# A third seven-product unit in tile 2, its x sums moved to the end of tile 1, and another PSUM bank for two value products of the prologue

## The chip, the cores and the metric

One Trainium2 chip, one core. The metric is device time of one execution in microseconds (us); medians are given with the lowest and highest run. A "profile" is one traced execution; its span is about 2 us shorter than the timed figure of the same run. Engines: PE is TensorE, DVE is VectorE, ACT is ScalarE, POOL is GpSimd.

## The reference

Shortened; x, the input of the second part, is the output of the first, put together over the heads.

```python
def _attn_ref(q, k, v):                       # 8 batches, 8 heads, 576 rows, 64 wide
    k_p = k.reshape(B, H, Sp, 8, D).mean(axis=3)      # keys and values pooled by 8
    v_p = v.reshape(B, H, Sp, 8, D).mean(axis=3)
    scores = scale * np.matmul(q, k_p.transpose(0, 1, 3, 2))
    ...                                               # softmax over the 72 pooled rows
    return np.matmul(attn, v_p)

def _moe_ref(x, w_in, w_out):                 # x: 4608 tokens x 512; d_ff = 2048
    h = x @ w_in
    g = h * (1.0 / (1.0 + np.exp(-h)))        # Silu
    return g @ w_out
```

## The kernel before

The tokens go through in nine tiles of 512. Tile t has an *up* phase (x @ w_in and Silu into `h_T`) and a *down* phase (times w_out), and beside the down phase the attention of batch t + 1. All matmuls are bf16, but for some of the warm-up. (Tile 4, and tile 0 for most groups, cut the 512 columns in two.)

An up phase has sixteen groups of 128 hidden columns. A plain group is four matmuls of 512 columns. A *unit* does four groups at once with Strassen's scheme: seven products of four 256-column matmuls, on sums of weights (`w_sum`, made once) and of tokens (`x_sum`, made per tile). Its outputs are put together by VectorE:

```python
elif n == "5":
    product(y, 5, "Q", True)
    tt(out=rr_sb, in0=ps[y, "Q"], in1=r_sb, op=ALU.add)
elif n == "1":
    product(y, 1, "R", True)
    tt(out=t_sb, in0=ps[y, "R"], in1=rr_sb, op=ALU.subtract)
...
elif n == "7":
    product(y, 7, "P", False)
    tt(out=c_sb[0], in0=ps[y, "P"], in1=t_sb, op=ALU.add)     # then a Silu from c_sb
```

The program fixes for each engine the order in which its instructions are issued, and the traces show VectorE keeping to it: in e4 below it sat idle for 1.73 us before one instruction, while sums that had run at this point of the tile in the kernel before stood behind it. `f_up` and `f_down` are lists of (step, piece of work): the piece is issued when the matmuls of the phase have come to that step:

```python
if t < 3:
    for n in U_X:
        f_up.append((0, lambda n=n: unit_x_sum(t, n)))        # x sums first thing in the tile
for n in (2, 5):
    h_at = 50 if t == B else 54 if t > 2 else 45
    f_up.append((h_at, lambda n=n: hidden_sum(n, 4, 8)))      # token sums of h_T for the down phase
...
else:                                                         # t > 1
    f_up.append((1, behind_x_sums))       # a GpSimd copy that reads x_sum: holds POOL until they are done
    f_up.append((1, lambda: pool_k(a)))   # two GpSimd adds
    ...
    f_up.append((2, lambda: pool_v(a)))   # two more
```

The kernel takes its PSUM tiles, into which the matmuls write, from two pools of banks: three (`mm`) and five (`at`). Each pair of value products of the prologue (the work before the first hidden matmul) takes one of each, each set of scores four of the five.

The softmax here doesn't subtract the row's maximum and nothing guards it: scores larger than these inputs give would overflow.

## Time and profile before

282.61 us (282.60 to 282.72, three runs). The first hidden matmul starts at 16.2 us and the rest of tile 0 lasts 34.9 us. Tile 0 has no unit, tile 1 one, tile 2 two, tiles 3 to 8 three.

### The profile page before, as it was taken

What the parts mean: (1) busy time and instruction counts of PE and PEld (TensorE: products, weight loads), DVE (VectorE), ACT (ScalarE), POOL (GpSimd) and SP (SyncE); (2) the same over time, 40 slices, a digit from 0 to 9 for tenths busy, and PEclk for the clock granted to TensorE, in tenths of its full rate; (3) what the DMA queues carried; (4) which work ended last, traced back from release to release, by engine and by line L of the source; (5) the groups of instructions that cost most, each with busy time, mean ns of one, the idle gap of its engine ahead of it and who ended that gap; (6) DMA issues with size and microseconds to landing.
All of it is one profiled execution on the core that took longest, in us unless ns stands there. A gap on an engine that the chain in (4) does not pass through costs nothing.

```text
span 280.5 us, 7088 instructions
## 1 busy us (share of the span) xinstructions
PE 275.4 (98%) x2853; PEld 201.4 (72%) x2853; DVE 218.2 (78%) x409; ACT 187.7 (67%) x365; POOL 98.7 (35%) x104
## 2 busy tenths in 40 slices
PE   8999999999999999999999999999999999999995
PEld 4448444556777578867888878787877778788684
DVE  4886746889887876897689768885888588966983
ACT  1688765668677776797579857984799578326700
POOL 8745217332138630863077106970640000000001
PEclk9999999999999999999999999999999999999999
DMA  7999999795659769569755944699610041004104
GB/s 210 284 260 238 210 325 171 227 197 94 148 72 203 200 108 170 129 181 132 138 132 154 135 65 121 141 144 139 160 26 2 0 105 49 0 11 109 33 4 148
DMA packets 31312, 37.70 MB, mean 134 GB/s; under 512 B 10352, under 2 KB 22256, under 8 KB 31280
## 3 DMA queue, kind: packets, MB, share of 16 engines
q0 software_dynamic: 23920, 27.03, 51.7%
q1 hardware_dynamic: 6928, 9.58, 12.4%
q10 hardware_dynamic: 432, 0.66, 0.6%
q8 instruction: 22, 0.36, 0.5%
q14 instruction: 10, 0.08, 0.1%
HBM read 36.70 MB, written 9.44 MB: 164 GB/s over the span
## 4 chain that ended last, share of the span: by engine, by line
PE 82%; DMA 12%; DVE 3%; issue 1%; ACT 1%; DVEq 0%
PE o_psP L645 15%; PE o_psQ L645 15%; PE hp_ps L537 13%; PE u_psP L477 10%; PE u_psQ L477 10%; PE o_psR L645 5%; DMA w_out_sb<-in_moe_w_out_dram 5%; DMA raw<-in_k_dram 4%; DMA q_bf<-in_q_dram 3%; PE u_psR L477 3%; PE sc_ps L340 3%; PE nu_ps L384 2%; PE warm_ps L694 2%; PE den_ps L358 2%; PE warm_ps L698 1%
## 5 line engine op out<-in xcount | busy, mean ns | idle before, releaser
L645 PEld LDWEIGHTS <-h_sum 128*128 128x128 bf16 x640 | 60.4, 98 | 13.1 <-DVE h_sum L605 2.7
L537 PE MATMUL hp_ps<-xT,w_in_sb 128*128 128x512 bf16 (+3 forms) x300 | 58.1, 337 | 0.1
L605 DVE TENSOR_TENSOR h_sum<-h_T 128x1024 bf16<-128x1024 bf16 (+1 forms) x72 | 51.9, 771 | 1.0 <-ACT h_T L543 1.0
L477 PEld LDWEIGHTS <-w_sum 128*128 128x128 bf16 x420 | 41.1, 98 | 7.7
L543 ACT ACTIVATE h_T<-hp_ps 128x512 bf16<-128x512 f32 (+2 forms) x71 | 36.3, 528 | 12.9 <-PE hp_ps L537 11.7
L348 ACT ACTIVATE es<-sc_ps 72x384 bf16<-72x384 f32 (+1 forms) x100 | 39.1, 470 | 8.8 <-PE sc_ps L340 8.7
L537 PEld LDWEIGHTS <-w_in_sb 128*128 128x128 bf16 x300 | 28.6, 98 | 18.4 <-issue 1.1
L485 ACT ACTIVATE h_T<-c_sb 128x512 bf16<-128x512 f32 x42 | 26.1, 627 | 4.9 <-DVE c_sb L509 4.3
L393 DVE TENSOR_TENSOR xT<-nu_ps,rec 128x384 bf16<-128x384 f32 (+1 forms) x50 | 24.0, 532 | 4.3 <-PE nu_ps L384 4.3
L645 PEld LDWEIGHTS <-h_T 128*128 128x128 bf16 x256 | 24.1, 98 | 4.5 <-issue 0.9
L549 POOL DMA_DIRECT2D out_dram<-o_sb x2 | 1.2, 618 | 68.3 <-issue 67.6
L367 ACT ACTIVATE lnd<-den_ps 128x384 f32<-128x384 f32 (+1 forms) x23 | 11.1, 484 | 19.7 <-PE den_ps L358 19.7
L190 POOL TENSOR_TENSOR raw<-raw 72x1024 f32<-72x1024 f32 x10 | 23.6, 2360 | 0.1
L500 DVE TENSOR_TENSOR t_sb<-u_psR,rr_sb 128x512 f32<-128x512 f32 x21 | 14.5, 692 | 6.7 <-PE u_psR L477 4.8
L494 ACT COPY r_sb<-u_psP 128x512 f32<-128x512 f32 x21 | 12.3, 584 | 10.1 <-PE u_psP L477 8.7
L263 DVE TENSOR_TENSOR raw<-raw 128x384 f32<-128x384 f32 (+3 forms) x20 | 12.4, 618 | 8.5 <-DMA raw<-in_v_dram 4.9
L645 PE MATMUL o_psP<-w_out_sb,h_sum 128*128 128x256 bf16 x128 | 17.7, 273 | 0.6 <-DVE h_sum L605 0.6
L477 PEld LDWEIGHTS <-w_in_sb 128*128 128x128 bf16 x168 | 16.1, 98 | 2.6
L497 DVE TENSOR_TENSOR rr_sb<-u_psQ,r_sb 128x512 f32<-128x512 f32 x21 | 14.3, 681 | 3.7 <-ACT r_sb L494 2.1
L509 DVE TENSOR_TENSOR c_sb<-u_psP,t_sb 128x512 f32<-128x512 f32 x21 | 14.4, 687 | 3.1 <-ACT h_T L485 1.4
L196 POOL COPY gate<-x_sum 1x1 bf16<-1x1 bf16 x5 | 0.9, 180 | 44.9 <-DVE x_sum L444 44.9
L645 PE MATMUL o_psQ<-w_sum,h_sum 128*128 128x256 bf16 x128 | 16.7, 273 | 0.0
(84 smaller groups left out, 518.6 us busy)
## 6 DMA issues: line engine op xcount, KB each, us to landing
out_dram<-o_sb SPq DMA_DIRECT2D x128, 64.0 KB, 1.8
raw<-in_k_dram POOLq DMA_DIRECT2D x10, 576.0 KB, 8.1
raw<-in_v_dram POOLq DMA_DIRECT2D x10, 576.0 KB, 7.8
q_bf<-in_q_dram POOLq DMA_DIRECT2D x6, 576.0 KB, 10.9
w_in_sb<-in_moe_w_in_dram POOLq DMA_DIRECT2D x8, 256.0 KB, 8.5
w_out_sb<-in_moe_w_out_dram POOLq DMA_DIRECT2D x4, 512.0 KB, 13.2
raw<-in_v_dram POOLq DMA_DIRECT2D x2, 768.0 KB, 11.0
raw<-in_k_dram POOLq DMA_DIRECT2D x1, 768.0 KB, 10.7
```

The costliest lines, as they stand in the source:

```text
L190: nc.gpsimd.tensor_add(out=raw[:, :, : 2 * D], in0=raw[:, :, : 2 * D], in1=raw[:, :, 2 * D :])
L348: nc.scalar.activation(es[:, s, :], sc[s], func=AF.Exp, scale=score_scale)
L393: nc.vector.tensor_mul(out=xT[:, 2 * g0 + c : 2 * (g0 + ng - 1) + c + 1 : 2, cols], in0=nu[c][:, :w].rearrange("r (g n) -> r g n", g=ng), ...
L477: nc.tensor.matmul(ps[y, bank][:, u, :], lhsT=w[:, kk, 128 * u : 128 * (u + 1)], rhs=x[:, kk, :], start=first and u == 0 and kk == 0, stop ...
L485: nc.scalar.activation(h_T[:, g : g + 2, j * NQ : (j + 1) * NQ], src, func=AF.Silu)
L497: tt(out=rr_sb, in0=ps[y, "Q"], in1=r_sb, op=ALU.add)
L500: tt(out=t_sb, in0=ps[y, "R"], in1=rr_sb, op=ALU.subtract)
L509: tt(out=c_sb[0], in0=ps[y, "P"], in1=t_sb, op=ALU.add)
L537: nc.tensor.matmul(hp_ps[:, r0:r1], lhsT=w_in_sb[:, kk, g * 128 : (g + 1) * 128], rhs=xT[:, kk, x0 : x0 + r1 - r0], start=(kk == 0), stop= ...
L543: nc.scalar.activation(h_T[:, g, n0 : n0 + n], hp_ps[:, :n], func=AF.Silu)
L605: nc.vector.tensor_tensor(out=h_sum[n][:, ks, :], in0=quarter(*a, ks), in1=quarter(*b, ks), op=op)
L645: nc.tensor.matmul(ps[b][:, c, :], lhsT=left(n, kt, c), rhs=W_OUT[n][:, kt, :], start=b not in begun, stop=kt == k1 - 1, skip_group_check= ...
```

## The change

Its intent: give tile 2 the third unit that tiles 3 to 8 have, with their whole schedule, and let the prologue's scores not wait for a bank.

```diff
-    numerators(0, part(1, 0), ("mm", "at"))
+    numerators(0, part(1, 0), ("mm", "mm"))
...
-            elif t > 2:
+            else:
                 items = []
                 for it in THREE[t // B].split(): ...          # the three-unit order
-            else:
-                items = ( ... two units ... )
-            if t < 3:
+            if t == 1:
                 for n in U_X:
                     f_up.append((0, lambda n=n: unit_x_sum(t, n)))
             for n in (2, 5):
-                h_at = 50 if t == B else 54 if t > 2 else 45
+                h_at = 50 if t == B else 54 if t > 1 else 45
...
-            q_at = [4, 14, 4, 8] if t > 2 else [15, 16, 17, 8] if t > 1 else ...
+            q_at = [4, 14, 4, 8] if t > 1 else ...
...
-        if 1 < t < B:
+        if 0 < t < B:
             for n in (4, 1, 3, 7, 6):
                 f_down.append((98 if t < B - 1 else 44, lambda n=n: unit_x_sum(t + 1, n)))
```

More of the change, by code (lines that the diff above doesn't have):

```diff
@@ L815 @@
                     items += [(("BCA".index(it[0])), it[1])] if it[0] in "ABC" else G(int(it[1]))
-            else:
-                items = (
-                    G(12, 13) + [(0, "251")] + G(14) + [(0, "43")] + G(15) + [(0, "76")]
-                    + [(1, "2")] + [(0, "hs")] + [(1, "51")] + G(0) + [(1, "43")] + G(1)
-                    + [(1, "7h6")] + G(2) + [(1, "s")] + G(3)
-                )
-            if t < 3:
+            if t == 1:
                 for n in U_X:
@@ L842 @@
         if a < B:
-            q_at = [4, 14, 4, 8] if t > 2 else [15, 16, 17, 8] if t > 1 else [24, 25, 26, 2] if t else [82, 84, 86, 88]
+            q_at = [4, 14, 4, 8] if t > 1 else [24, 25, 26, 2] if t else [82, 84, 86, 88]
             if t == 0:
@@ L867 @@
             for n in range(4):
-                f_to = f_down if t and n >= (2 if t > 2 else 3) else f_up
+                f_to = f_down if t and n >= (2 if t > 1 else 3) else f_up
                 f_to.append((q_at[n], lambda n=n: q_transpose(a, n % 2, n // 2)))
```

## The prediction

> **What bounds the kernel now.** I read four things in this order: the page's busy shares, the waits of TensorE, a table of windows cut at the nine token tiles, and the timelines of the two places that the change touches. The page first:
>
> ```profile
> PE 275.4 (98%) x2853; PEld 201.4 (72%) x2853; DVE 218.2 (78%) x409; ACT 187.7 (67%) x365; POOL 98.7 (35%) x104
> ```
>
> 98% of a 280.5 us span alone proves little, because matmul ends are modelled and overlap. So I ask for TensorE's waits:
>
> ```profile
> engine line waited for: us in total, times, longest us
> PE warm_ps L694 <- DVE warm L713: 1.2, 1, 1.2
> PE o_psP L645 <- DVE h_sum L605: 0.6, 1, 0.6
> ```
>
> Only two waits are left. The first is the start of the program. The second is one single event, and the PE timeline puts it at 97.63 us, in the second half of tile 2. Starts of consecutive matmuls say the rest: a 256-column product starts every 0.109 us and a 512-column one every 0.216 us, and apart from changes of operation nothing departs from this for long. So from about 16 us to the end the kernel is a queue on TensorE, and a change is worth what it takes out of that queue.
>
> I then cut the span where the matmuls of a new token tile begin (columns: stretch and its length, then busy us and count for PE, PEld, DVE, ACT, POOL; clock, DMA share, GB/s). The rows are tiles 1, 2, 3 and 4:
>
> ```profile
> 51.10:81.35 30.25, 30.20 (x318) 20.19 (x317) 26.41 (x60) 21.94 (x41) 9.17 (x9) 1.00 0.68 142
> 81.35:111.62 30.27, 29.62 (x314) 21.39 (x312) 23.41 (x39) 21.41 (x42) 12.98 (x10) 1.00 0.87 166
> 111.62:140.35 28.73, 28.73 (x326) 22.66 (x324) 23.31 (x42) 22.12 (x43) 12.65 (x10) 1.00 0.74 146
> 140.35:169.10 28.75, 28.75 (x342) 24.18 (x340) 23.28 (x42) 22.11 (x43) 11.90 (x9) 1.00 0.60 121
> ```
>
> This table carries the prediction. Tile 2 takes 30.27 us, and tiles 3 and 4, which have three seven-product units already, take 28.73 and 28.75. (Some matmul records are missing, so counts are not compared.) Tile 2 has 0.65 us in which PE was not busy, tile 3 none.
>
> Why does tile 2 wait? Its PE, DVE and POOL timelines, then DVE at the same place of tile 3:
>
> ```profile
> 97.63 1.05 PE L645 MATMUL o_psP<-w_out_sb,h_sum 128*128 128x256 bf16 x8 [0.65 <-DVE h_sum L605]
> 99.48 0.67 PE L358 MATMUL den_ps<-es,ones 72*32 72x384 bf16 x4
> ```
> ```profile
> 90.76 3.33 DVE L605 TENSOR_TENSOR h_sum<-h_T 128x1024 bf16<-128x1024 bf16 x2
> 94.01 0.68 DVE L509 TENSOR_TENSOR c_sb<-u_psP,t_sb 128x512 f32<-128x512 f32 x1
> ```
> ```profile
> 89.48 2.37 POOL L190 TENSOR_TENSOR raw<-raw 72x1024 f32<-72x1024 f32 x1
> 91.94 1.60 POOL L193 TENSOR_TENSOR vp<-raw 72x512 bf16<-72x512 f32 x1
> ```
> ```profile
> 123.53 4.29 DVE L605 TENSOR_TENSOR h_sum<-h_T 128x1024 bf16<-128x1024 bf16 x7
> ```
>
> In tile 2 two hidden sums took 3.33 us, 1.67 each; in tile 3 seven took 4.29, 0.61 each. The slow pair lies beside GpSimd's two pooling adds. Behind it the unit's last c_sb starts at 94.01; ScalarE sat idle 2.03 us for that c_sb, finished its last Silu at 96.84, and the sums that the down product needs began at 96.88. That is the 0.65 us. The two ragged denominators at 99.48 (0.67 us against 0.35 elsewhere) are its tail, since the exponentials come after those Silus on ScalarE.
>
> **What the Trainium skill says.** "SBUF — State Buffer", section "Who interferes with whom": a VectorE instruction with two SBUF inputs contends with a GpSimd instruction that reads SBUF, and the one that comes second is blocked. A hidden sum is such an instruction, and the trace agrees: 1.67 us beside the adds against 0.61 alone. "TensorE: Matmul & The Clock Gate", section "Wait — 56ns, not 53.3ns?": a warm matmul costs N / 2.4 GHz and about 2.5 ns, that is 109.2 ns for 256 columns and 215.8 for 512. The trace agrees (0.109 and 0.216; granted clock 1.00 in every tile). "PSUM — Partial Sum Buffer", section "PSUM bank collisions raise a hardware error": a bank must be guarded by semaphores whole, not by address. So a matmul into a recycled bank waits for its last reader; the prologue shows that below.
>
> **The change part by part.**
>
> *1. Third unit in tile 2.* A unit replaces four hidden groups of four 512-column matmuls: 16 x 0.2158 = 3.45 us. It has seven products of four 256-column matmuls: 28 x 0.1092 = 3.06 us. TensorE is saved 0.39 us. The two up phases say the same: tile 2 goes from 81.35 to its first down product at 94.50, 13.15 us; tile 3 from 111.62 to 124.37, 12.75 us; 0.40 apart. It adds four VectorE operations of about 0.69 us (rr, t and two c) and one ScalarE copy of 0.58; the four plain Silus become four of 0.60 to 0.63. None of this lies on PE's path if the order holds, and the order is tile 3's, where the same load of 23.3 us VectorE and 22.1 us ScalarE runs with no PE wait.
>
> *2. Hidden sums from step 45 to step 54.* They now follow the last c_sb, as in tile 3, some 11.9 us after the tile's start: 93.3 on the clock of before. GpSimd's adds end at 93.54 now, but they hang behind a gate that waits for the x sums (POOL was idle 4.07 us for it). With the x sums a part of tile 1 that gate opens about 1.45 us earlier, so the adds should end near 91.8. Sums and adds no longer meet. So the wait (0.65 as idle, 0.81 by start-to-start: 0.918 instead of 0.107) goes, and with it the ragged denominators, 0.33. Parts 1 and 2 together: 0.40 + 0.81 + 0.33 = 1.54 us, just what the table gives: 30.27 - 28.73 = 1.54.
>
> *3. x sums at the end of tile 1.* Five VectorE operations, 1.75 us for all, unchanged in number. They now stand between the last xT products (done 80.79) and the last output sum, which moves from 81.55 to about 82.4. It holds an output bank, which the next tile's later groups need; tile 3 starts with the same order (xT done 0.56 us before its first matmul, as also here) and shows no wait. PE time: 0.
>
> *4. Prologue.* The second value product pair goes into two banks of the three, so that it takes no bank of the five. The rows of now (ScalarE, PE, ScalarE):
>
> ```profile
> 14.54 1.30 ACT L348 ACTIVATE es<-sc_ps 72x288 bf16<-72x288 f32 x4
> ```
> ```profile
> 15.12 1.17 PE L340 MATMUL sc_ps<-qT,kz 32*72 32x288 bf16 x8
> ```
> ```profile
> 16.24 1.30 ACT L348 ACTIVATE es<-sc_ps 72x288 bf16<-72x288 f32 x4 [0.40 <-PE sc_ps L340]
> 17.56 1.28 ACT L403 ACT_TABLE_LOAD   x1
> ```
>
> Eight score matmuls took 1.17 us where the same eight take 0.45 elsewhere. The starts of the first four are 0.17, 0.30 and 0.30 us apart, in step with the four exponentials that free their banks (each new one 0.30 after the last): bank for bank they wait for all four. With one more bank free they wait for the first three alone, so the fourth starts one exponential, 0.30 us, earlier. The hidden products behind it (16.23) follow, and so do the exponentials, the table load and the Silus that a later value product waits for: everything moves by about 0.29 us. Its own operands allow it: the xT products it needs end at 16.02 and are first used after the denominators; the first input-weight halves have landed by 15.1, as the queue's waits show.
>
> Sum: 282.61 - 1.54 - 0.29 = **280.78 us**.
>
> **The rivals.**
> *The prologue's gain is absorbed.* In tile 0 data from memory come at fixed times: the value rows are summed after a 4.9 us DMA wait, and the output weights land just in time. If one of these were the limit, PE would wait there and the 0.29 would go. For: the chain of waits runs through DMA up to 46 us. Against: PE shows no wait there; value sums are done 1.9 to 2.5 us before PE uses them, and the last quarter of the output weights, issued at 26.54 and given the longest landing of 15.7 us, is there at 42.24, about 0.6 us before its use. The result would be 281.1.
> *Only the arithmetic goes, a wait stays.* If the sums still meet GpSimd's adds (the load between the adds, or a late value row, holds these), or tile 1's fuller VectorE (26.4 us against 23.3) hands on a delay, tile 2 keeps part of its 1.14 us and the result is 281.3 to 281.9. Against: in tile 1 VectorE sat idle 0.92 and 0.76 us near its end, so it is not behind.
> *The new order makes PE wait*, for x sums or an output bank: 283 at worst. Against: the x sums end near 82.4, and their first product comes some 2.2 us after the tile's start, at 83.5, as in tile 3.
>
> **Range and chances.** The centre is 280.8 because two separate readings of tile 2 (parts, and tile 3 as a twin) agree. The range runs from 280.4 (all of it and some rounding) to 281.5 (prologue absorbed and part of the wait kept); 2% would be 5.65 us, over three times the whole gain, so "faster by over 2%" has 1%, slower 1%, within 98%.
>
> **What would show each step.** Tile 2, between first matmuls, should last 28.7 to 28.8 us, and its up phase 12.75. TensorE's wait for h_sum should be gone from the waits, VectorE's hidden sums of tile 2 should last 0.61 us each, and the gate should run about 1.4 us earlier within its tile. The eight scores should take about 0.87 us, the first hidden product should start near 15.94, and tile 1 should begin near 50.8 instead of 51.1. I am wrong on the prologue if tile 1 still begins at 51.1, and wrong on tile 2 if a PE wait for h_sum, x_sum or u_ps is left or new.

## More of the kernel before

The experiments ran in three sets on three chips (e1, e2, e3, e7; e4, e5, e6, e8; e9 to e12), each set with the kernel before run beside it.

## The result

280.56 us (280.25 to 281.55, six runs) against 282.61 of before (282.29 to 282.82, six runs). The ratio is 0.9933, 95% interval 0.9917 to 0.9950: the mean time of the runs of one kernel over that of the other's in the same rounds, so not quite the ratio of the medians. The interval is clear of 1, and the change is, as forecast, well within 2%. A later control, in another set of runs, gave 280.68 and 0.9942.

The waits of TensorE in the changed kernel (same columns as before):

```profile
PE warm_ps L694 <- DVE warm L713: 1.2, 1, 1.2
PE kz_ps L285 <- DVE k L267: 0.8, 1, 0.8
```

The wait for `h_sum` is gone. The second line lies before 8 us, where the first key rows come in; it differs from run to run. Tiles 1, 2 and 3 by windows:

```profile
50.94:81.17 30.23, 30.17 (x318) 20.22 (x317) 26.95 (x62) 21.95 (x41) 9.18 (x9) 1.00 0.71 146
81.17:109.90 28.73, 28.73 (x326) 22.65 (x324) 23.30 (x42) 22.12 (x43) 12.67 (x10) 1.00 0.90 176
109.90:138.63 28.73, 28.73 (x326) 22.64 (x324) 23.30 (x42) 22.12 (x43) 12.68 (x10) 1.00 0.72 141
```

Tile 2 is now its sister's twin in length and in VectorE, ScalarE and GpSimd time. GpSimd in tile 2, then VectorE:

```profile
82.35 0.18 POOL L196 COPY gate<-x_sum 1x1 bf16<-1x1 bf16 x1 [3.64 <-DVE x_sum L444]
...
87.88 2.39 POOL L190 TENSOR_TENSOR raw<-raw 72x1024 f32<-72x1024 f32 x1
90.34 1.27 POOL L193 TENSOR_TENSOR vp<-raw 72x512 bf16<-72x512 f32 x1
```
```profile
93.07 4.29 DVE L605 TENSOR_TENSOR h_sum<-h_T 128x1024 bf16<-128x1024 bf16 x7
```

The gate runs 1.18 us after the tile's start instead of 2.63. The adds end at 91.61, the sums begin at 93.07 and take 0.61 each. The prologue, on TensorE:

```profile
14.99 0.88 PE L340 MATMUL sc_ps<-qT,kz 32*72 32x288 bf16 x8
15.80 0.42 PE L537 MATMUL hp_ps<-xT,w_in_sb 128*128 128x288 bf16 x2
```

The eight scores take 0.88 us for 1.17, and hidden work starts 0.81 us after the first score, not 1.11. But tile 1 starts at 50.94, only 0.18 us earlier than in the profile of before. Where did the rest of that 0.3 go? TensorE's timeline in tile 0's down phase, before and then after:

```profile
41.79 1.68 PE L572 MATMUL o_ps<-w_out_sb,h_T 128*128 128x512 bf16 x7
43.31 0.34 PE L303 MATMUL v_ps<-v,shifts 128*128 128x64 bf16 x6
```
```profile
41.36 1.94 PE L572 MATMUL o_ps<-w_out_sb,h_T 128*128 128x512 bf16 x7
43.14 0.34 PE L303 MATMUL v_ps<-v,shifts 128*128 128x64 bf16 x6
```

The same seven matmuls take 0.26 us more. By single starts it is one gap: 0.476 us from 42.23 to 42.71 where 0.216 is the pace, and the matmul behind it is the first that waits for the semaphore of the last quarter of w_out. It does not show among the waits, because the modelled end of the matmul before covers 0.16 of it and the view leaves out the 0.10 that remain. The last quarter's landing is the longest of the four in the view of `w_out_sb`, before and then after:

```profile
DMA to landing us min/median/max: 11.9/13.2/15.7
```
```profile
DMA to landing us min/median/max: 11.9/13.3/16.1
```

It was issued at 26.54 and 26.57, so it was there at 42.22 before (used at 42.88) and at 42.67 after (used at 42.71). So TensorE, now earlier, ran into a transfer.

Summed over the two profiled runs: 0.18 us before tile 1, none in tile 1, 1.54 in tile 2, none in tiles 3 to 7, and 0.15 at the very end (see the last section but one): 1.87 us, the difference of the spans (280.53 and 278.66). Of the 0.18, 0.13 was there before the eight scores began (14.99 against 15.12), so it is not the bank's doing.

### The profile page after: what moved, and what is told of

The parts are those of the page before. It is cut to its first block, busy times and chain, and to the rows that moved or that the text cites. A ratio compares the mean times of both kernels' runs of the same rounds, so it can differ in the third digit from the quotient of the medians.

```text
span 278.7 us, 7121 instructions
## 1 busy us (share of the span) xinstructions
PE 273.3 (98%) x2865; PEld 201.9 (72%) x2865; DVE 218.7 (78%) x413; ACT 188.4 (68%) x366; POOL 98.7 (35%) x104
## 4 chain that ended last, share of the span: by engine, by line
PE 81%; DMA 12%; POOL 2%; DVE 2%; issue 1%; DVEq 0%; POOLq 0%
PE o_psP L645 16%; PE o_psQ L645 16%; PE hp_ps L537 12%; PE u_psP L477 10%; PE u_psQ L477 10%; DMA w_in_sb<-in_moe_w_in_dram 6%; DMA w_out_sb<-in_moe_w_out_dram 6%; PE o_psR L645 5%; PE u_psR L477 3%; PE sc_ps L340 3%; PE nu_ps L384 2%; PE den_ps L358 2%; DVE w_sum L623 1%; POOL q_bf L133 1%; DVE xT L393 1%
## 5 line engine op out<-in xcount | busy, mean ns | idle before, releaser
L537 PE MATMUL hp_ps<-xT,w_in_sb 128*128 128x512 bf16 (+3 forms) x284 | 54.1, 334 | 0.1
L605 DVE TENSOR_TENSOR h_sum<-h_T 128x1024 bf16<-128x1024 bf16 (+1 forms) x72 | 49.7, 742 | 0.0
L477 PEld LDWEIGHTS <-w_sum 128*128 128x128 bf16 x440 | 43.1, 98 | 7.8
L543 ACT ACTIVATE h_T<-hp_ps 128x512 bf16<-128x512 f32 (+2 forms) x67 | 33.8, 524 | 11.5 <-PE hp_ps L537 10.5
L537 PEld LDWEIGHTS <-w_in_sb 128*128 128x128 bf16 x284 | 27.1, 98 | 17.1 <-issue 1.1
L485 ACT ACTIVATE h_T<-c_sb 128x512 bf16<-128x512 f32 x44 | 27.5, 628 | 3.1 <-DVE c_sb L509 2.4
L500 DVE TENSOR_TENSOR t_sb<-u_psR,rr_sb 128x512 f32<-128x512 f32 x22 | 15.2, 692 | 7.0 <-PE u_psR L477 5.5
L494 ACT COPY r_sb<-u_psP 128x512 f32<-128x512 f32 x22 | 12.9, 584 | 10.0 <-PE u_psP L477 8.7
L477 PEld LDWEIGHTS <-w_in_sb 128*128 128x128 bf16 x176 | 16.9, 98 | 2.3
L509 DVE TENSOR_TENSOR c_sb<-u_psP,t_sb 128x512 f32<-128x512 f32 x22 | 15.1, 688 | 2.7 <-PE u_psP L477 1.0
L512 DVE TENSOR_TENSOR c_sb<-u_psQ,t_sb 128x512 f32<-128x512 f32 x22 | 15.1, 687 | 2.4 <-PE u_psQ L477 2.3
```

Of the source, the lines that this page charges most:

```text
L477: nc.tensor.matmul(ps[y, bank][:, u, :], lhsT=w[:, kk, 128 * u : 128 * (u + 1)], rhs=x[:, kk, :], start=first and u == 0 and kk == 0, stop ...
L485: nc.scalar.activation(h_T[:, g : g + 2, j * NQ : (j + 1) * NQ], src, func=AF.Silu)
L512: tt(out=c_sb[1], in0=ps[y, "Q"], in1=t_sb, op=ALU.add)
L537: nc.tensor.matmul(hp_ps[:, r0:r1], lhsT=w_in_sb[:, kk, g * 128 : (g + 1) * 128], rhs=xT[:, kk, x0 : x0 + r1 - r0], start=(kk == 0), stop= ...
L543: nc.scalar.activation(h_T[:, g, n0 : n0 + n], hp_ps[:, :n], func=AF.Silu)
L605: nc.vector.tensor_tensor(out=h_sum[n][:, ks, :], in0=quarter(*a, ks), in1=quarter(*b, ks), op=op)
```

## The experiments

All are edits of the kernel before or of the changed kernel. Theory A: tile 2's wait came from GpSimd's adds beside two VectorE sums, a unit itself is worth 0.4 us, and the prologue's gain is mostly lost to the last quarter of the output weights. Rivals are named with each.

The times of the kernel before beside each set: 282.36, 282.38 and 282.35 us. A tile's length is taken between first matmuls in the profile.

| run | edit | us (median) | ratio, 95% interval | tile 2, us |
|---|---|---|---|---|
| e7 | before, x sums moved alone | 281.32 | 0.9964 (0.9946 to 0.9982) | 29.13 |
| e4 | before, sums later alone | 281.57 | 0.9974 (0.9960 to 0.9988) | 29.18 |
| e5 | before, one GpSimd add left out | 281.12 | 0.9962 (0.9947 to 0.9977) | 29.13 |
| e6 | changed, x sums put back | 280.85 | 0.9946 (0.9933 to 0.9960) | 28.91 |
| e1 | changed, prologue put back | 280.78 | 0.9940 (0.9925 to 0.9955) | 28.74 |
| e2 | before, prologue alone | 282.17 | 0.9991 (0.9976 to 1.0006) | 30.31 |
| e3 | changed, w_out's quarter earlier | 281.31 | 0.9961 (0.9947 to 0.9975) | 28.74 |
| e8 | changed, value selection earlier | 280.35 | 0.9933 (0.9921 to 0.9946) | 28.73 |
| e12 | changed, control | 280.68 | 0.9942 (0.9930 to 0.9955) | 28.74 |
| e9 | e8 and weight sums later | 280.30 | 0.9925 (0.9912 to 0.9939) | 28.73 |
| e10 | e8 and the quarter in two halves | 280.26 | 0.9925 (0.9913 to 0.9938) | 28.74 |
| e11 | all three | 280.25 | 0.9925 (0.9913 to 0.9938) | 28.74 |

### What the wait in tile 2 was

**e7: the x sums moved, nothing else.**

```diff
-            if t < 3:
+            if t == 1:
...
-        if 1 < t < B:
+        if 0 < t < B:
```

> The kernel before with tile 2's x sums at the end of tile 1, and nothing else. Theory A (the wait in tile 2 came from GpSimd's adds beside the two hidden sums, and the gate behind the x sums sets when the adds run): the adds run 1.4 us earlier and end near 91.9, only the first hidden sum still meets them, the pair takes 2.0 to 2.4 us instead of 3.33, TensorE's wait of 0.65 us shrinks to 0 to 0.2 and the time falls by 0.8 to 1.15 us, to 281.5 to 281.8. Rival C (the order of the sums ahead of c_sb was the cause, or the arithmetic of the third unit all that counts): the wait stays at 0.5 us or more and the time falls by under 0.3 us.

Tile 2 fell from 30.27 to 29.13 us, with two units and the old order of the hidden sums. VectorE and GpSimd in it:

```profile
90.96 2.17 DVE L605 TENSOR_TENSOR h_sum<-h_T 128x1024 bf16<-128x1024 bf16 x2
93.06 0.68 DVE L509 TENSOR_TENSOR c_sb<-u_psP,t_sb 128x512 f32<-128x512 f32 x1
```
```profile
90.72 1.26 POOL L193 TENSOR_TENSOR vp<-raw 72x512 bf16<-72x512 f32 x1
```

The first sum still meets the last add, the second no longer: 2.17 us for the pair instead of 3.33. That 1.16 is, to 0.02, the wait and its tail (0.81 + 0.33). The time fell by about 1.0 us. Rival C, that only the order or the arithmetic counts, fails.

**e5: the suspected add taken away.** Wrong on purpose for one batch; order, units and x sums as before.

```diff
-        pool_rows(st["vp"], st["v_raw"])
+        pool_rows(st["vp"], st["v_raw"], first=b != 3)      # leaves out the 2.4 us add in tile 2
```

> The kernel before, wrong on purpose for one batch: GpSimd's first value add in tile 2 (2.4 us) left out, so its second add runs near 88.8 to 90.1 and nothing stands beside the two hidden sums. Order on VectorE, units and x sums as before. Theory A: the two hidden sums take 0.61 us each, the wait goes, tile 2 lasts about 29.13 us as with the x sums moved, the time falls by 1.0 to 1.2 us. Rival C (order or work, not contention): the sums still take over 1.2 us each or the wait stays, and tile 2 lasts 30.2.

```profile
90.26 1.28 DVE L606 TENSOR_TENSOR h_sum<-h_T 128x1024 bf16<-128x1024 bf16 x2
```
```profile
88.99 1.30 POOL L194 TENSOR_TENSOR vp<-raw 72x512 bf16<-72x512 f32 x1
```

(One source line was added, so 605 is 606.) GpSimd's second add now ends as the sums begin. The pair takes 1.28 us in its old place, and tile 2 lasts 29.13, the same as in e7. With GpSimd's add gone and nothing else edited, the wait is gone: this settles the cause.

**e4: the sums moved behind the last c_sb, nothing else.**

```diff
-                h_at = 50 if t == B else 54 if t > 2 else 45
+                h_at = 50 if t == B else 54 if t > 1 else 45
```

> The kernel before with tile 2's two early hidden sums moved behind the last c_sb (step 54 for 45), nothing else: two units, x sums at the start of tile 2, GpSimd's adds where they were. Theory A (sums beside the adds hold c_sb back, c_sb holds the last Silus back): c_sb starts near 92.4 instead of 94.0, the last Silu ends near 95.8, TensorE's wait falls to 0 to 0.2 us, tile 2 lasts 29.1 to 29.4 us and the time falls by 0.8 to 1.15. Rival C (the wait comes from having too little product work left behind the last Silus in a two-unit tile, whatever the sums do): tile 2 stays at 30.0 or more.

```profile
93.19 0.69 DVE L509 TENSOR_TENSOR c_sb<-u_psP,t_sb 128x512 f32<-128x512 f32 x1 [1.73 <-PE u_psP L477]
93.80 0.68 DVE L512 TENSOR_TENSOR c_sb<-u_psQ,t_sb 128x512 f32<-128x512 f32 x1
94.39 4.29 DVE L605 TENSOR_TENSOR h_sum<-h_T 128x1024 bf16<-128x1024 bf16 x7
```

c_sb now waits for its product (1.73 us idle) and not for VectorE; the last Silu ends at 96.03, 14.1 us after the tile's start instead of 15.5. Tile 2: 29.18, a hair above e7. The time fell by 0.7 (means) to 0.8 us (medians), the low end of what was expected or just under it; the profiled run lost 0.91 us to a transfer before tile 1 (below). (My clock figures in the expectation were off by the 0.6 us by which this run was late; the tile length is the test.)

**e6: the third unit without the move.**

```diff
-            if t == 1:
+            if t < 3:
...
-        if 0 < t < B:
+        if 1 < t < B:
```

> The changed kernel with tile 2's x sums put back to the start of tile 2, so the third unit without the move. Theory A: the gate runs 1.4 us later than in the changed kernel, GpSimd's adds end near 93.1 on the changed kernel's clock, where the first hidden sum starts (93.07 there, later here), so they hardly meet; tile 2 lasts 28.7 to 29.1 us, that is 0 to 0.4 above the changed kernel: either of the two edits removes the wait and the gains do not add. Rival D (the move is needed: x sums late make TensorE wait for x_sum, or the sums still meet the adds): a wait for x_sum, t_sb or h_sum of 0.5 us or more in tile 2.

Tile 2: 28.91, which is 0.17 above the changed kernel, inside the range. The hidden sums are at 0.61 us each. The 0.17 is one gap, TensorE's and then VectorE's lines:

```profile
84.09 0.60 PE L477 MATMUL u_psR<-x_sum,w_sum 128*128 128x256 bf16 x4
84.70 0.60 PE L477 MATMUL u_psQ<-x_sum,w_in_sb 128*128 128x256 bf16 x4
```
```profile
82.29 1.76 DVE L444 TENSOR_TENSOR x_sum<-xT 128x512 bf16<-128x512 bf16 x5
83.97 0.68 DVE L497 TENSOR_TENSOR rr_sb<-u_psQ,r_sb 128x512 f32<-128x512 f32 x1
```

Four 256-column matmuls take 0.437 us of pace; here the next group comes 0.61 later. It writes the bank u_psQ that rr_sb reads, and the profile puts the wait of its first matmul down to rr_sb, which stands behind the x sums and ends at 84.65. So rival D is right that late x sums make TensorE wait, though for the sum behind them and not for themselves, and wrong on the size.

Together: from 30.27, either moving the x sums or moving the hidden sums buys 1.1 us. That the two gains do not add follows from both ending the same meeting; both at once were run only with the third unit, where the move still brought 0.17, by the other wait just shown. The unit with its order brings tile 2 to 28.91, and the x sums moved as well to 28.73. The arithmetic of the unit alone, e7 to the changed kernel, is 29.13 - 28.73 = 0.40 us.

### What became of the prologue's gain

**e1 and e2: each part alone.** One line, in either direction:

```diff
-    numerators(0, part(1, 0), ("mm", "mm"))
+    numerators(0, part(1, 0), ("mm", "at"))      # e1; e2 is the reverse, on the kernel before
```

> The changed kernel with the prologue put back (second value products in one bank of the three and one of the five). Theory A (the two parts are separate, and the prologue's gain is mostly lost to the last quarter of the output weights): tile 2 still lasts 28.73 us between first matmuls, the hidden product starts near 16.2 again, tile 1 starts 0.15 to 0.2 us later than in the changed kernel, and the time is 0.15 to 0.2 us above it, near 281.0 against 282.6 of before (ratio 0.9945). Rival B (the prologue's 0.29 us reaches the end): 0.29 to 0.4 us above the changed kernel.

> The kernel before with the prologue's bank alone changed. Theory A: the eight scores take 0.88 us instead of 1.17 and hidden products start 0.3 us earlier, but TensorE waits about 0.26 us for the last output-weight quarter near 42.4 us, so tile 1 starts 0.0 to 0.2 us earlier than 51.11 and the time falls by that, to 282.4 to 282.6. Rival B: no such wait, and the time falls by 0.29 us or more, to 282.3.

In time neither part of this question is resolved: e1 lies 0.22 above the first runs of the changed kernel and 0.10 above its control, and e2's interval includes 1. My expectations by the clock missed too: in both runs the scores began earlier (14.69 and 14.60) than in the profiles at hand, so "tile 1 starts later than in the changed kernel" failed in e1 by this alone. What can be compared is inside one run: from the first of the eight scores to the first matmul of tile 1, and the extra gap at the first matmul on w_out's last quarter (start to start less 0.216).

| run | bank of the prologue | scores to tile 1, us | extra gap at w_out | less the gap |
|---|---|---|---|---|
| before | old | 35.99 | 0 | 35.99 |
| e7 | old | 35.98 | 0 | 35.98 |
| e5 | old | 35.97 | 0 | 35.97 |
| e1 | old | 36.06 | 0.14 | 35.92 |
| e4 | old | 36.83 | 0.91 | 35.92 |
| changed | new | 35.95 | 0.26 | 35.69 |
| e2 | new | 36.02 | 0.34 | 35.68 |
| e6 | new | 36.22 | 0.54 | 35.68 |
| e12 (control) | new | 36.38 | 0.69 | 35.69 |
| e8, e9, e10 | new | 35.67 | 0 | 35.67 |

Without the gap the new bank is worth 0.3 us, as worked out. With it, anything from 0.3 down to less than nothing. In the eleven profiles with this transfer in its old place and whole, it landed between 42.14 us (e5) and 43.44 (e4), and TensorE came or would have come to it between 42.06 (e2) and 43.08 (e7; where it waited, the start before plus 0.216). So it is a toss-up in the old kernel too (e1 and e4 have the old bank):

```profile
42.39 0.59 PE L572 MATMUL o_ps<-w_out_sb,h_T 128*128 128x512 bf16 x2 [0.17 <-DMA w_out_sb<-in_moe_w_out_dram]
```
```profile
43.33 0.59 PE L572 MATMUL o_ps<-w_out_sb,h_T 128*128 128x512 bf16 x2 [0.52 <-DMA w_out_sb<-in_moe_w_out_dram]
```

(e2 and the control e12. The idle shown is shorter than the gap, as the matmul before is drawn 0.38 us long and not 0.216.) In the control the quarter's landing, the longest of the four, is the longest of all runs:

```profile
DMA to landing us min/median/max: 12.0/13.3/16.8
```

Why the same transfer lands up to 1.3 us apart is not settled here. The chip alone is not the reason, as on one chip it came at 42.14 (e5) and at 43.44 (e4); the DMA row of both kernels' pages stands at nine tenths from 7 to 49 us.

**e3: the quarter loaded earlier.**

```diff
     load_slots(nc.gpsimd, 1, "v", 0, 3)
+    load_w_out(3)
     load_slots(nc.gpsimd, 1, "v", 3, 4)
     load_slots(nc.gpsimd, 1, "v", 4, 5)
-    load_w_out(3)
```

> The changed kernel with the last output-weight quarter issued before the last two pieces of the value rows and not after. Theory A: the start-to-start gap of 0.476 us at 42.23 becomes 0.216, tile 1 starts 0.26 us earlier (near 50.7), and the time falls by about 0.25 us, to 280.3. Rival B (the value rows, now later, make TensorE wait, or the gap has another cause): the gap stays or a wait for v_ps or its sums of 0.3 us or more appears, and the time does not fall.

The gap at w_out went, and rival B came true beside it: the later value rows made TensorE wait.

```profile
44.46 0.34 PE L303 MATMUL v_ps<-v,shifts 128*128 128x64 bf16 x6 [0.97 <-DVE vp L310]
```

A net loss: 0.63 to 0.75 us above the changed kernel's two medians. It shows that the gap hangs on that transfer, and that the place in the queue was already contested.

**e8: fill the gap with work that is ready.** The value rows of the first slots are ready about 2 us before TensorE uses them, so their six small matmuls can go ahead of the product that waits.

```diff
-  f_down.append((37 + 3 * j, lambda j=j: select_v(1, j, "at")))
+  f_down.append((35 + 5 * j, lambda j=j: select_v(1, j, "at")))
```

> The changed kernel with tile 0's first six value-selecting matmuls (0.18 us, their data ready at 40.8) put ahead of the first product that needs the last output-weight quarter. Theory A (TensorE waits there for memory at 42.4 to 42.7): 0.1 to 0.18 us of that wait is filled, tile 1 starts up to 0.18 us earlier relative to the landing (wait at that product 0.1 or less), the time falls by 0.0 to 0.2 us, to 280.4 to 280.6. Rival B (the gap there has another cause): the gap stays and the time does not fall.

```profile
42.34 0.34 PE L303 MATMUL v_ps<-v,shifts 128*128 128x64 bf16 x6
42.52 1.24 PE L572 MATMUL o_ps<-w_out_sb,h_T 128*128 128x512 bf16 x5
```

Five products in 1.24 us, so there is no gap, though the quarter landed at 42.48, after TensorE was free at 42.34; 35.67 us to tile 1. The median is 0.2 below the first runs of the changed kernel, in another set, so the gain in time rests on the runs below.

### A version that beats both

> The changed kernel itself, as a control beside the next three. All theories: 280.4 to 280.8 us; tile 2 at 28.73; a wait for the last output-weight quarter of 0 to 0.7 us that differs from run to run, since that quarter landed between 42.4 and 43.5 us in the runs so far.

> The changed kernel with the value selection ahead of the output-weight wait, and with four of the eight output-weight sums of VectorE behind the last x products of tile 0. Theory A: the wait of 0.22 us at the second matmul of tile 1 (for x products that stood behind those sums) goes, so that tile 1's two first matmuls are 0.216 apart; the time is 0.1 to 0.4 us below the changed kernel. Rival: the x sums, now later, make TensorE wait in tile 1 (x_sum or kz_ps), and nothing is won.

> The changed kernel with the value selection early and the last output-weight quarter loaded as two halves. Theory A (TensorE waits for memory there): the first half lands up to 1 us earlier than the quarter, no wait for output weights is left, the prologue's 0.3 us arrives whole (35.67 us from the eight scores to tile 1 as in the run with the early selection), and the time is 0.0 to 0.3 us below the changed kernel. Rival: one more transfer delays the key rows behind it and a wait for kz_ps appears in tile 1.

> All three edits together. Theory A: the gains add, 35.4 to 35.5 us from the eight scores to tile 1, the time 0.2 to 0.5 us below the changed kernel and the lowest of all, near 280.2. Rival: as in the two before.

```diff
-            (3, 0, f_down, 52, (0, PW)),      # e9, e11: four of tile 0's eight weight sums ...
+            (3, 0, f_down, 57, (0, PW)),      # ... behind its last x products
...
-        cs = slice(c * KG // 4, (c + 1) * KG // 4)
+        n = 2 if c == 3 else 1                # e10, e11: the last quarter of w_out in two transfers
+        for i in range(n):
+            cs = slice((n * c + i) * KG // (4 * n), (n * c + i + 1) * KG // (4 * n))
```

Beside the control (five runs each, 280.46 to 281.22) e9 ran in 280.11 to 280.39, e10 in 279.89 to 280.54, e11 in 279.96 to 280.68. The means are 280.72, 280.27, 280.24 and 280.24, so 0.44 to 0.47 us below the changed kernel, far within 2%. The control's profiled run, with its 0.69 us gap, is its slowest (281.22, the other four 280.46 to 280.73) and lifts its mean; by medians the gain is 0.38 to 0.43. Only e9's runs all lie below the control's. None of the three had a gap at w_out; but in e9's profiled run the quarter had landed at 42.36, 0.5 us before its use, so there the early selection was not put to the test, as it was in e8. In e10 the first half landed at 41.28 and was used at 42.41. The weight sums moved (e9) took away the 0.22 us wait of tile 1's second matmul, but a gap of 0.16 came at 53.27, behind ScalarE: tile 1 fell by 0.07 us only. I had also looked for that gain before tile 1, where it cannot show, so the 35.4 to 35.5 us of e11 did not come (35.62). What the halves add to the early selection was not told apart (e8 and e10 are of different sets), and e9, e10 and e11 are equal within their noise.

## Why the prediction was right

*The bound.* "A queue on TensorE" held: the gains that the profiles show are stretches that left that queue. (Two rows of the table were cut a little early: between first matmuls tile 1 lasts 30.23 and tile 4 28.78 us.)

*Part 1, the unit (0.39 to 0.40 us).* Right: 0.40 between e7 and the changed kernel. (0.2158 and 0.1092 are estimates from the page's formula; the trace's 0.216 and 0.109 give the same.) The up phase takes 12.75 us (81.17 to 93.92), the figure given.

*Part 2, the wait (1.14 us).* Right in size, and the mechanism is shown by e5, not only argued. One half of the explanation was too narrow: I put "hidden sums from step 45 to 54" as the edit that ends the meeting, with the earlier gate as its helper. Either of the two does it alone (e4 and e7).

*Part 3, the x sums.* "PE time: 0" for moving them, and so it was in tile 1 (30.23 both). Left out was what they buy with the third unit: 0.17 us (e6), through the table's twin already in the total.

*Parts 1 and 2 by the twin.* 30.27 - 28.73 = 1.54 was predicted and is what the two profiles show.

*Part 4, the prologue (0.29 us).* The mechanism was right (0.88 us for the scores, predicted 0.87), the gain at its place 0.3. But "tile 1 should begin near 50.8" came out as 50.94, and that close only by scores that began 0.13 us earlier: the rival "the prologue's gain is absorbed" came true for most of the gain in that profile. The mis-sized term is the slack of the last output-weight quarter, "about 0.6 us before its use": the rival took it that data "come at fixed times", and I took the landing of one profile for the landing of all. Over the runs it comes between 0.9 us before (e7) and 0.9 us after (e4) the time at which TensorE wants it. Of 0.29 us some 0.04 (0.30 less 0.26) was left in the profiled run of the changed kernel; the rest of the 0.18 at tile 1 is that run's earlier scores, not the change.

*The total.* 280.8 against 280.56 and 280.68: that it came so close is partly luck. In the two profiles 0.25 of the prologue's 0.29 us was lost, and made up by two things that were not foreseen: 0.15 us in the last tile, and the 0.13 us by which the scores of that run began earlier. The profiles differ by 1.87 us, the medians by 2.05.

## What to carry to other kernels

When repeated stages differ, take the best as the forecast for the others, and take the stage's wait apart before crediting the arithmetic: here three quarters of what "a third unit" brought was a VectorE and GpSimd meeting that a shift of some lines ends as well. Before you count a gain early in a kernel, look up the next thing that comes at a fixed time, a transfer above all, and measure its slack over several runs, since one profile can show a tie as a pass. Where such a tie exists, work that is ready can be put in front of it, which cost nothing here, while moving the transfer forward hurt.

## What the runs showed that I had not expected

- In the last tile, where no instruction was changed, the stretch from its first matmul to the end took 28.49 to 28.52 us in the five kernels with two units in tile 2 (before, e2, e4, e5, e7) and 28.36 to 28.38 in the nine with three. In the profile of before the down phase starts with three gaps of 0.05 to 0.08 us that the changed kernel lacks; a later gap is 0.04 longer there. The banks may be handed out in another order after the third unit; no run tested this, so the cause is open.
- A gap behind a 512-column matmul shows about 0.17 us too short among the waits (0.17 for 0.34 in e2, 0.52 for 0.69 in the control), and the gap of 0.26 in the changed kernel does not show at all. Starts are the measure.

## What the Trainium skill lacked or had wrong

- "TensorE: Matmul & The Clock Gate", section "Back-to-back issue gap", gives about 131 ns per 512-column matmul for a sustained stream of weight loads and matmuls, and says that the formula over-counts there. In these runs, a stream of just such pairs (2853 weight loads for 2853 matmuls in the profile of before), it is the formula that holds: 0.216 us start to start, in every tile that has matmuls of this width (tile 4 has none).
- "ScalarE: Activation LUTs", section "What ACT_TABLE_LOAD costs", puts a switch of table sets at about 2.66 us, a load of 1.28 and a drain of 1.38. The trace of before agrees on the load (1.28 us) but shows no drain beside it: the exponentials end at 17.54, the load runs from 17.56 to 18.84, and the first Silu starts at 18.85.
- "SBUF — State Buffer", section "Who interferes with whom", says that whoever comes second is blocked until the whole instruction of the first is over. That fits: the sum issued at 90.76 beside an add that ended at 91.86 ended at 92.42, 0.56 later, about its own length of 0.61; in e7 a sum beside an add that ended at 91.98 ended at 92.53, 0.55 later. The page speaks of operations measured slower, but does not say that a trace draws the blocked time inside the instruction and not as idle time: 1.67 us instead of 0.61, so that the chain behind it looks like slow VectorE work.
- No page that I read says how much one and the same transfer may vary from run to run when the queues are full: 15.7 to 16.8 us from issue to landing here, over eleven profiles.
